# Gated unit of an adaLN block: TensorE and VectorE in source order, the weights' low parts one product behind, the last rows' steps beside the products without down products

## The chip, the cores and the metric

The kernel runs on one core of a Trainium2 chip. The metric is the time of one execution on the device, in microseconds. The engines are TensorE (PE, with its weight loads PEld), VectorE (DVE), ScalarE (ACT), GpSimd (POOL) and SyncE (SP), which here only issues transfers. Each engine works through a queue of its own in order; a semaphore makes an instruction wait for another engine or for a transfer.

## The reference

One block of a transformer with conditioning, on 2048 rows of 576 columns in fp32:

```python
mod = (silu(c) @ w_mod).reshape(c.shape[0], 6, 1, -1)
h = layernorm(x) * (1 + ca) + sa
x = x + ga * attention(h, wqkv, wo)                 # 32 heads of 18, softmax
h = layernorm(x) * (1 + cb) + sb
x = x + gb * ((sigmoid(h @ w_gate) * (h @ w_up)) @ w_down)      # 576 -> 4608 -> 576
```

The last line is the gated unit, the only part that the change touches.

## The kernel before

Attention comes first, up to about 1599 us of the profile. The gated unit fills the rest. It works on two halves of 1024 rows. Each half runs over 18 blocks of 256 of the 4608 inner columns.

**Products.** In a block, gate and up projections together would be eight products of quarter size (two halves of the rows, of the 576 columns and of the block); a scheme of Strassen's kind makes seven of them, in the order `ORDER = (1, 6, 2, 7, 5, 4, 3)` (L43). So the list `seq` (L1074) has 2 x 18 x 7 = 252 products, and `n % 7` is the place in the block, 0 to 6. fp32 values are kept as a high and a low part in fp32r; `product` (L1024) runs 7 matmuls (high by high, high by low, low by high) for the gate and 7 for the up projection, 14 matmuls of 128x512. The activation operands `X[s]` lie in SBUF for the whole half.

**Weights.** `weights_operand` (L991) makes a product's weight tile `w`: GpSimd forms sums and differences of the raw quarters into S1, S2, S3 (L1008), ScalarE casts the high part (L1019), VectorE subtracts for the low part (L1020, L1021), and SP's queue sends the finished tile to the DRAM tensor `ws` (L1022). In the second half the tile is only read back from `ws` (L998). `prepare(n)` (L1094) is called `LOOK = 3` products ahead, and the pool of `w` has four slots. It also loads the raw weights of later blocks.

**What follows a product.** Place 0 (product 1) goes into two banks "x", and ScalarE copies them to p1 (L1206). Place 1 (product 6) goes into "bg" and "bu", and VectorE adds p1 for u2 (L1212). Place 2 (product 2) accumulates on place 0's banks, and `gate` (L1033) follows. Place 3 (product 7) accumulates on bg and bu; L1223 adds for u3. Place 4 (product 5) takes two banks "x", L1228 adds, and a gate follows; place 5 (product 4) accumulates on bg and bu, L1234 and a gate; place 6 (product 3) accumulates on place 4's banks, L1239 and a gate. There are three banks "x", so the next block's place 0 takes a bank that L1239 has to read first. A gate is a chain over two engines: sigmoid on ScalarE (L1037 or L1040), multiply on VectorE (L1038 or L1041), cast of the high part on ScalarE (L1043), subtraction of the low part on VectorE (L1044).

**Down products.** Behind places 1 and 3 stands `down` (L1051) for the block before: eight groups of six matmuls of 288 columns, each into one of three banks "d", each read by one add of VectorE into Oa (L1068).

**Last rows.** Rows 1024 to 2047 still lack the last columns of attention's output product, their layer norm and the activation operands of the second half. The generator `last_rows` (L1108) does this in steps, each up to a `yield`, beside the first half: four transposes and splits of VectorE (L1124 to L1136), products with two adds (L1147, L1150), statistics (L156, L157), scales (L163 to L177, with a square root on ScalarE), normalized rows (L695, with a copy on GpSimd at L698), transposes whose results go to the DRAM tensor `hs` (`ln_spill`, L703), and last the sums and the high and low parts of the operands (`operand_parts`, L717, with the cast L726, the subtractions L728 and L733 and the transfer to `xs`). A step follows every second product (L1241). These steps use the banks "d" as well.

**Who sets the order.** A planner in the framework orders each engine's queue at compile time, by source order as a priority and by its own durations. Inside `tc.manual_schedule(engines=...)` the named engines keep the source order. In the gated unit TensorE alone is named, from product `ORDERED = 56` on, that is from block 8 of the first half (L1197). VectorE, ScalarE, GpSimd and SP are ordered by the planner all the time.

Of the kernel before, what the change touches and what calls it, by code (L numbers as in the profile page):

```python
# [15 lines left out]
F32 = mybir.dt.float32  # L16
# [7 lines left out]
P = 128  # L24
S = 2048
D = 576
# [7 lines left out]
HALF = D // 2  # L34
# [8 lines left out]
ORDER = (1, 6, 2, 7, 5, 4, 3)  # L43
# [5 lines left out]
SINGLE = (0, 1, 16, 17, 18, 19, 20, 27, 28, 29)  # L49
SIDES = ((0, 0), (0, 1), (1, 0), (1, 1))  # L50
TURNED = ((0, 1), (0, 0), (1, 1), (1, 0)), ((0, 1), (1, 1), (0, 0), (1, 0))
ORDERED = 56


@with_exitstack
def tile_block(ctx, tc, x_in, wqkv, wo, w_gate, w_up, w_down, c_in, w_mod, out):
# [102 lines left out]
    def ln_scales(pool, mv, rs):  # L159
        for _ in ln_scales_steps(pool, mv, rs):  # L160
            pass
# [826 lines left out]
    sums = ctx.enter_context(tc.tile_pool(name="sums", bufs=1))  # L988
    wdp = ctx.enter_context(tc.tile_pool(name="wdp", bufs=1))

    def weights_operand(st, k):  # L991

        w = wgp.tile([P, 2, 5, P], F32R, name="w")
        st["w", k] = w
        kept = ws[st["b"], ORDER.index(k)]
        flat = w.rearrange("p v a c -> p (v a c)").bitcast(F32)
        if st["half"] == 1:
            nc.sync.dma_start(flat, kept.bitcast(F32))  # L998
            return
        raw = st["raw"]  # L1000
        A11, A12 = raw[0][:, :, :, 0:P], raw[1][:, :, :, 0:P]
        A21, A22 = raw[0][:, :, :, P:256], raw[1][:, :, :, P:256]

        def put(name, a, b, op):
            if name not in st:
                st[name] = sums.tile([P, 2, 3, P], F32, name=name)
            for v in range(2):
                nc.gpsimd.tensor_tensor(st[name][:, v], a[:, v], b[:, v], op=op)  # L1008

        if k == 6:  # L1010
            put("S1", A21, A22, ALU.add)
            put("S2", st["S1"], A11, ALU.subtract)
            put("S3", A11, A21, ALU.subtract)
        elif k == 3:
            put("S2", A12, st["S2"], ALU.subtract)
        src = {1: A11, 2: A12, 4: A22}.get(k)
        if src is None:
            src = st[{5: "S1", 6: "S2", 7: "S3", 3: "S2"}[k]]
        nc.scalar.copy(w[:, :, 0:3, :], src)  # L1019
        nc.vector.tensor_sub(w[:, :, 3:5, :], src[:, :, 0:2, :], w[:, :, 0:2, :].bitcast(F32))  # L1020
        nc.vector.tensor_sub(w[64:P, :, 2, :], src[64:P, :, 2, :], w[64:P, :, 2, :].bitcast(F32))  # L1021
        nc.sync.dma_start(kept.bitcast(F32), flat)  # L1022

    def product(st, k, acc, first):  # L1024
        s, w = ORDER.index(k), st["w", k]
# [66 lines left out]
        return blocks[half, b]  # L1092

    def prepare(n):  # L1094
        if n < len(seq):
            weights_operand(block(n), seq[n][2])
            at = n % 7
            if at in (1, 3):
                load(n // 7 + 1, at // 2)
# [8 lines left out]
    def last_rows():  # L1108
# [5 lines left out]
        with tc.tile_pool(name="fin", bufs=1, side="right") as pool:  # L1114
            w = pool.tile([P, 2, 2, D], F32R, name="w")
            nc.gpsimd.dma_start(w, wod)
            for t0 in (0, 4):
                od = pool.tile([P, 4, 256], F32, name="od")
                nc.sync.dma_start(od[:, :, 0:192], oend[:, t0 : t0 + 4, :])
                nc.sync.dma_start(od[:, :, 192:256], oend[:, t0 : t0 + 4, 128:192])  # L1120
                yield
                pt = psum()
                for j in range(4):
                    nc.tensor.transpose(pt[:, j * P : (j + 1) * P], od[:, j, 0:P], ident)  # L1124
                oh = pool.tile([P, 512], F32R, name="oh")
                ol = pool.tile([P, 512], F32R, name="ol")
                nc.vector.tensor_copy(oh, pt)
                nc.vector.tensor_sub(ol, pt, oh.bitcast(F32))
                pt = psum()
                for j in range(4):  # L1130
                    nc.tensor.transpose(pt[:, j * P : (j + 1) * P], od[:, j, P:256], ident)
                om = pool.tile([P, 512], F32R, name="om")
                omh = pool.tile([P, 512], F32R, name="omh")
                nc.vector.tensor_copy(om[0:64], pt[0:64])
                nc.vector.tensor_copy(omh[64:P], pt[64:P])
                nc.vector.tensor_sub(om[64:P], pt[64:P], omh[64:P].bitcast(F32))  # L1136
                yield
                for j in range(4):
                    rows = slice(j * P, (j + 1) * P)
                    xt = pool.tile([P, D], F32, name="xt", bufs=2)  # L1140
                    nc.sync.dma_start(xt, x1p[:, t0 + j, :])
                    for h in range(2):
                        cols = slice(h * HALF, (h + 1) * HALF)
                        acc = psum()
                        ts_ = ((oh, 0, 0), (oh, 1, 0), (ol, 0, 0), (om, 0, 1), (om, 1, 1))
                        for n, (a, i, k) in enumerate(ts_):
                            nc.tensor.matmul(  # L1147
                                acc[:, :HALF], a[:, rows], w[:, i, k, cols], start=n == 0, stop=n == 4
                            )
                        nc.vector.tensor_add(xt[:, cols], xt[:, cols], acc[:, :HALF])  # L1150
                    nc.sync.dma_start(x1d[:, t0 + j, :], xt)
                    yield
# [4 lines left out]
        with tc.tile_pool(name="zp2", bufs=1, side="right") as zp:  # L1157
            for ch in (2, 3):
                zs = []
                for t in range(4 * ch, 4 * ch + 4):  # L1160
                    z = zp.tile([P, 2, 384], F32, name="z", bufs=4)
                    x1 = z[:, :, 0:HALF]
                    for g in range(2):
                        nc.sync.dma_start(z[:, g, 0:HALF], x1d[:, t - 8, g * HALF : (g + 1) * HALF])
                    ln_stats(zp, x1, mv2[:, t, :])
                    zs.append(z)
                four = slice(4 * ch, 4 * ch + 4)
                ln_scales(zp, mv2[:, four, :], rs2[:, four])
                for j, z in enumerate(zs):
                    ln_rows(z, 4 * ch + j, z[:, :, 0:HALF], nc.vector)  # L1170
                yield
                yield from ln_spill(zs, ch, psum, zp, modulated)
        with tc.tile_pool(name="xop2", bufs=2) as pool:
# [7 lines left out]
            for i in range(3):  # L1181
                blocks = get()
                for (g, r), t in zip(((0, 0), (0, 1), (1, 0), (1, 1)), blocks):
                    cols = slice(HW + r * 512, HW + (r + 1) * 512)
                    nc.sync.dma_start(t, hs[g, i, :, cols])
                yield from operand_parts(1, i, blocks, parts, nc.scalar.copy, nc.vector, nc.sync)

    def banks(*names):
# [6 lines left out]
    before = None  # L1195
    for n, (hf, b, k) in enumerate(seq):
        if n == ORDERED:  # L1197
            manual.enter_context(tc.manual_schedule(engines={mybir.EngineType.PE}))
        prepare(n + LOOK)
        st = block(n)  # L1200
        if k == 1:
            st["a"] = banks("x", "x")
# [33 lines left out]
        else:  # L1236
# [1 line left out]
            for v in range(2):  # L1238
                nc.vector.tensor_add(half(st["u2"], v), st["c"][v], half(st["u2"], v))  # L1239
            gate(st, st["u2"], 0, 1)  # L1240
        if n >= 5 and n % 2:  # L1241
            next(rows2, None)
        if before is not None and k in (6, 7):
            down(before, k - 6)
        if k == 3:
# [34 lines left out]
```

## Time and profile before

| what | us |
|---|---|
| time, median of 3 runs (2929.81 to 2933.68) | 2929.95 |
| the profiled execution's own time | 2929.86 |
| its span in the profile | 2927.5 |
| start of the gated unit's first product | 1599.17 |
| TensorE busy | 2848.3 |
| VectorE busy | 2218.6 |
| ScalarE busy | 1581.4 |
| GpSimd busy | 649.4 |

A row of a timeline has the start, the duration, the engine, the line, the operation, the output and input tiles (buffer numbers left out), the shapes and the count; a bracket at its end gives the engine's idle time before it and whom it waited for. In the wait list a row names who waited for whom, the total in us, the number of waits and the longest. In a list of groups, the figures behind the bar are busy us, mean ns of one, and the idle time before.

### The profile page before, as it was taken

How to read it: one execution, taken by the hardware profiler on the slowest of the kernel's cores; microseconds unless marked ns; L12 is line 12 of the kernel's file. 1: busy time of each engine (PE TensorE's matmuls, PEld its weight loads, DVE VectorE, ACT ScalarE, POOL GpSimd, SP SyncE). 2: the span in 40 equal slices, each digit the busy share in tenths (PEclk: the TensorE clock that was granted, in tenths of full speed). 3: DMA queues.
4: the chain of work that ended last, by engine and by line, in shares of the span. 5: the costliest groups of instructions: out<-in, count | busy, mean ns of one | idle time of the engine just before them, and what ended most of it. 6: DMA issues, size and time to landing. Idle time of an engine off the chain costs nothing.

```text
span 2927.5 us, 46356 instructions
## 1 busy us (share of the span) xinstructions
PE 2848.3 (97%) x17141; PEld 1879.6 (64%) x17141; DVE 2218.6 (76%) x4023; ACT 1581.4 (54%) x2955; POOL 649.4 (22%) x829
## 2 busy tenths in 40 slices
PE   7999999999999999999999899999999999999998
PEld 6964333333444444444443788877888888888888
DVE  7277888888899988999982878789777555555555
ACT  3216889999987778998788333333332111111111
POOL 3122014544213110761102222233221100000000
PEclk9999999999999999999999999999999999999999
DMA  5344124333212110222125866677556844554443
GB/s 180 120 157 128 52 76 140 133 120 123 84 56 76 35 56 23 101 98 66 52 87 177 284 216 234 231 277 247 207 201 233 301 170 167 167 168 167 159 159 136
DMA packets 136745, 429.25 MB, mean 147 GB/s; under 512 B 18884, under 2 KB 56520, under 8 KB 124232
## 3 DMA queue, kind: packets, MB, share of 16 engines
q1 hardware_dynamic: 120472, 344.99, 35.0%
q0 software_dynamic: 16048, 81.31, 7.9%
q8 instruction: 135, 2.21, 0.3%
q14 instruction: 90, 0.74, 0.1%
HBM read 267.77 MB, written 157.95 MB: 145 GB/s over the span
## 4 chain that ended last, share of the span: by engine, by line
PE 82%; DVE 7%; ACT 4%; DMA 3%; issue 3%; SPq 1%; POOL 0%; POOLq 0%; ACTq 0%; DVEq 0%
PE o L548 16%; PE d L1064 14%; PE x L1028 12%; PE s L446 11%; PE s L927 10%; PE bu L1028 4%; PE bg L1028 4%; PE s L274 4%; ACT p L931 3%; PE s L325 2%; PE s L685 2%; DVE mx L452 1%; DVE w L1020 1%; DMA B<-hs 1%; PE s L572 1%
## 5 line engine op out<-in xcount | busy, mean ns | idle before, releaser
L452 DVE TENSOR_REDUCE mx<-s 128x1 f32<-128x512 f32 x1696 | 1076.6, 684 | 126.3 <-PE s L446 108.3
L931 ACT ACTIVATE p<-s 128x512 f32<-128x512 f32 x2048 | 1068.4, 610 | 146.7 <-PE s L446 75.2
L446 PE MATMUL s<-k,q 54*128 54x512 f32 x1920 | 608.4, 451 | 12.2 <-ACT p L931 6.6
L548 PE MATMUL o<-p,vaug 128*32 128x512 f32 x4096 | 554.8, 607 | 0.5 <-ACT p L931 0.4
L927 PE MATMUL s<-q,k 56*128 56x512 f32 x1920 | 552.6, 425 | 1.3 <-DMA q<-mrows 0.8
L1064 PE MATMUL d<-wd,hh 128*128 128x288 f32 x2304 | 468.3, 297 | 20.8 <-DVE Oa L1068 20.2
L927 PEld LDWEIGHTS s<-q,k 56*128 56x128 f32 x1920 | 260.5, 186 | 295.2 <-DVE mx L452 184.7
L446 PEld LDWEIGHTS s<-k,q 54*128 54x128 f32 x1920 | 273.6, 184 | 250.3 <-ACT p L931 172.3
L1064 PEld LDWEIGHTS d<-wd,hh 128*128 128x128 f32 x2304 | 373.4, 188 | 35.6 <-DVE Oa L1068 26.4
L1068 DVE TENSOR_TENSOR Oa<-Oa,d 128x288 f32<-128x288 f32 x576 | 256.0, 452 | 125.5 <-PE d L1064 120.3
L1064 PE MATMUL d<-wd,hl 128*128 128x288 f32 x1152 | 340.7, 296 | 0.0
L1028 PE MATMUL x<-k,w 128*128 128x512 f32 x1008 | 242.4, 390 | 4.7 <-DVE u L1239 2.4
L1040 ACT ACTIVATE u<-u 128x512 f32<-128x512 f32 x72 | 45.5, 632 | 318.3 <-DVE u L1228 312.1
L1064 PEld LDWEIGHTS d<-wd,hl 128*128 128x128 f32 x1152 | 216.9, 188 | 0.0
L1028 PEld LDWEIGHTS x<-k,w 128*128 128x128 f32 x1008 | 186.7, 188 | 42.5 <-DVE u L1239 3.5
L548 PEld LDWEIGHTS o<-p,vaug 128*32 128x32 f32 x4096 | 83.4, 108 | 163.9 <-issue 151.4
L1037 ACT ACTIVATE sg<-x 128x512 f32<-128x512 f32 x36 | 21.5, 599 | 304.3 <-PE x L1028 304.3
L1070 POOL DMA_DIRECT2D out_dram<-Oa x16 | 8.7, 543 | 606.0 <-DVE Oa L1068 606.0
L455 ACT ACTIVATE over<-s 128x512 f32<-128x512 f32 x176 | 105.1, 597 | 33.5 <-PE s L446 28.4
L1028 PE MATMUL x<-big,w 128*128 128x512 f32 x504 | 120.6, 390 | 1.0 <-issue 1.0
L1028 PE MATMUL x<-w,w 128*128 128x512 f32 x504 | 121.0, 390 | 0.0
L457 DVE CUSTOM_DVE_ANT_0 over<-s,over 128x512 f32<-128x512 f32 x176 | 120.2, 683 | 0.3
(232 smaller groups left out, 3605.1 us busy)
## 6 DMA issues: line engine op xcount, KB each, us to landing
ws<-w SPq DMA_DIRECT2D x126, 640.0 KB
w<-ws SPq DMA_DIRECT2D x126, 640.0 KB
wd<-wds SPq DMA_DIRECT2D x36, 1152.0 KB
k<-kd SPq DMA_DIRECT2D x60, 360.0 KB
wds<-w POOLq DMA_DIRECT2D x18, 1152.0 KB, 4.5
k<-kd SPq DMA_DIRECT2D x60, 180.0 KB
w<-in_B_w_down_dram POOLq DMA_DIRECT2D x18, 576.0 KB, 4.3
q<-qd SPq DMA_DIRECT2D x64, 144.0 KB
```

The source lines that it names most:

```text
L274: nc.tensor.matmul(acc, w, hT[:, t, cols], start=n == 0, stop=n == len(ts_) - 1)
L325: nc.tensor.matmul(acc[:, 0:HALF], hT[:, k, rows], w, start=n == 0, stop=n == len(ts_) - 1,)
L446: nc.tensor.matmul(sp, qs[rows, qt * P : (qt + 1) * P], ks[rows, at * 512 : (at + 1) * 512], start=True, stop=True,)
L452: nc.vector.tensor_reduce(to, sp, axis=AX.X, op=ALU.max)
L455: nc.scalar.activation(over, sp, AF.Relu)
L457: nc.vector.tensor_tensor_reduce(out=over, in0=sp, in1=over, scale=1.0, scalar=LOWEST, op0=ALU.add, op1=ALU.max, accum_out=mx[:, h * n + q ...
L548: nc.tensor.matmul(acc[32 * j : 32 * j + 32, :], vaug[:, kt, (2 * p + h) * VW : (2 * p + h) * VW + 32], probs[2 * c + h], start=kt == 0, s ...
L927: nc.tensor.matmul(sT, ks[rows, kcols], qs[rows, c * 512 : (c + 1) * 512], start=True, stop=True)
L931: state["exp"] = nc.scalar.activation(pr, sT, AF.Exp, scale=SCALE)
L1028: nc.tensor.matmul(acc[v], w[:, v, a, :], X[s][:, b, :], start=first and n == 0, stop=n == 6, skip_group_check=not first,)
L1064: nc.tensor.matmul(acc[:, :HALF], a[:, f, rows], w[:, f, cols], start=n == 0, stop=n == 5)
L1068: nc.vector.tensor_add(Oa[:, t, cols], Oa[:, t, cols], acc[:, :HALF])
```

## The change

Four edits. (1) From product 7 on (block 1 of the first half) TensorE and VectorE both keep the source order; before, TensorE alone did, from product 56. (2) `weights_operand` is split: `weights_high` does the sums and the cast three products ahead, as before, and `weights_low` does VectorE's subtractions and the transfer to `ws` one product later, at the head of the next `prepare`. (3) A step of `last_rows` is taken ahead of the product at places 0, 4, 5 and 6, from product 7 on, and no longer behind every second product; at these places no down products follow. (4) Inside `last_rows` the loads of `x1p` are issued one step ahead, the loads of z and of the blocks from `hs` become steps of their own, and statistics, scales and normalized rows become separate steps, so that there are 56 steps in place of 47.

```diff
--- before.py
+++ after.py
@@ -49,7 +49,8 @@
 SINGLE = (0, 1, 16, 17, 18, 19, 20, 27, 28, 29)
 SIDES = ((0, 0), (0, 1), (1, 0), (1, 1))
 TURNED = ((0, 1), (0, 0), (1, 1), (1, 0)), ((0, 1), (1, 1), (0, 0), (1, 0))
-ORDERED = 56
+ORDERED = 7
+ROWS_FROM = 7
 
 
 @with_exitstack
@@ -988,7 +989,7 @@
     sums = ctx.enter_context(tc.tile_pool(name="sums", bufs=1))
     wdp = ctx.enter_context(tc.tile_pool(name="wdp", bufs=1))
 
-    def weights_operand(st, k):
+    def weights_high(st, k):
 
         w = wgp.tile([P, 2, 5, P], F32R, name="w")
         st["w", k] = w
@@ -1017,9 +1018,18 @@
         if src is None:
             src = st[{5: "S1", 6: "S2", 7: "S3", 3: "S2"}[k]]
         nc.scalar.copy(w[:, :, 0:3, :], src)
+        st["src", k] = src
+
+    def weights_low(st, k):
+
+        if st["half"] == 1:
+            return
+        w, src = st["w", k], st["src", k]
         nc.vector.tensor_sub(w[:, :, 3:5, :], src[:, :, 0:2, :], w[:, :, 0:2, :].bitcast(F32))
         nc.vector.tensor_sub(w[64:P, :, 2, :], src[64:P, :, 2, :], w[64:P, :, 2, :].bitcast(F32))
-        nc.sync.dma_start(kept.bitcast(F32), flat)
+        nc.sync.dma_start(
+            ws[st["b"], ORDER.index(k)].bitcast(F32), w.rearrange("p v a c -> p (v a c)").bitcast(F32)
+        )
 
     def product(st, k, acc, first):
         s, w = ORDER.index(k), st["w", k]
@@ -1092,8 +1102,10 @@
         return blocks[half, b]
 
     def prepare(n):
+        if 0 < n <= len(seq):
+            weights_low(block(n - 1), seq[n - 1][2])
         if n < len(seq):
-            weights_operand(block(n), seq[n][2])
+            weights_high(block(n), seq[n][2])
             at = n % 7
             if at in (1, 3):
                 load(n // 7 + 1, at // 2)
@@ -1135,10 +1147,15 @@
                 nc.vector.tensor_copy(omh[64:P], pt[64:P])
                 nc.vector.tensor_sub(om[64:P], pt[64:P], omh[64:P].bitcast(F32))
                 yield
-                for j in range(4):
+                xts = []
+                for j in range(-1, 4):
+                    if j < 3:
+                        xts.append(pool.tile([P, D], F32, name="xt", bufs=2))
+                        nc.sync.dma_start(xts[-1], x1p[:, t0 + j + 1, :])
+                    if j < 0:
+                        continue
                     rows = slice(j * P, (j + 1) * P)
-                    xt = pool.tile([P, D], F32, name="xt", bufs=2)
-                    nc.sync.dma_start(xt, x1p[:, t0 + j, :])
+                    xt = xts[j]
                     for h in range(2):
                         cols = slice(h * HALF, (h + 1) * HALF)
                         acc = psum()
@@ -1159,13 +1176,15 @@
                 zs = []
                 for t in range(4 * ch, 4 * ch + 4):
                     z = zp.tile([P, 2, 384], F32, name="z", bufs=4)
-                    x1 = z[:, :, 0:HALF]
                     for g in range(2):
                         nc.sync.dma_start(z[:, g, 0:HALF], x1d[:, t - 8, g * HALF : (g + 1) * HALF])
-                    ln_stats(zp, x1, mv2[:, t, :])
                     zs.append(z)
+                yield
+                for j, z in enumerate(zs):
+                    ln_stats(zp, z[:, :, 0:HALF], mv2[:, 4 * ch + j, :])
                 four = slice(4 * ch, 4 * ch + 4)
-                ln_scales(zp, mv2[:, four, :], rs2[:, four])
+                yield from ln_scales_steps(zp, mv2[:, four, :], rs2[:, four])
+                yield
                 for j, z in enumerate(zs):
                     ln_rows(z, 4 * ch + j, z[:, :, 0:HALF], nc.vector)
                 yield
@@ -1183,6 +1202,7 @@
                 for (g, r), t in zip(((0, 0), (0, 1), (1, 0), (1, 1)), blocks):
                     cols = slice(HW + r * 512, HW + (r + 1) * 512)
                     nc.sync.dma_start(t, hs[g, i, :, cols])
+                yield
                 yield from operand_parts(1, i, blocks, parts, nc.scalar.copy, nc.vector, nc.sync)
 
     def banks(*names):
@@ -1195,8 +1215,10 @@
     before = None
     for n, (hf, b, k) in enumerate(seq):
         if n == ORDERED:
-            manual.enter_context(tc.manual_schedule(engines={mybir.EngineType.PE}))
+            manual.enter_context(tc.manual_schedule(engines={mybir.EngineType.PE, mybir.EngineType.DVE}))
         prepare(n + LOOK)
+        if n >= ROWS_FROM and n % 7 in (0, 4, 5, 6):
+            next(rows2, None)
         st = block(n)
         if k == 1:
             st["a"] = banks("x", "x")
@@ -1238,8 +1260,6 @@
             for v in range(2):
                 nc.vector.tensor_add(half(st["u2"], v), st["c"][v], half(st["u2"], v))
             gate(st, st["u2"], 0, 1)
-        if n >= 5 and n % 2:
-            next(rows2, None)
         if before is not None and k in (6, 7):
             down(before, k - 6)
         if k == 3:
```

## The prediction

> **What bounds the kernel now.** I read the page's shares of the engines first, then a table by stage (stretch, length, busy PE, PEld, DVE, ACT, POOL, granted clock, DMA).
>
> ```profile
> span 2927.5 us, 46356 instructions
> PE 2848.3 (97%) x17141; PEld 1879.6 (64%) x17141; DVE 2218.6 (76%) x4023; ACT 1581.4 (54%) x2955; POOL 649.4 (22%) x829
> ...
> 1600.00:1700.00 100.00, 91.68 (x496) 79.00 (x495) 76.80 (x129) 29.87 (x43) 26.84 (x25) 1.00 0.81 274
> 1900.00:2000.00 100.00, 90.99 (x490) 79.52 (x489) 84.81 (x136) 38.06 (x60) 36.06 (x28) 0.98 0.80 279
> 2400.00:2600.00 200.00, 200.00 (x1107) 177.78 (x1106) 113.07 (x196) 35.12 (x58) 0.00 (x0) 1.00 0.51 170
> ```
>
> TensorE is the bound. It has holes in the gated unit's first half and none in the second, so the change, which touches this unit alone, can win only what the first half loses. The timeline says how much that is.
>
> ```profile
> 2500.06 3.35 PE L1028 MATMUL x<-w,w 128*128 128x512 f32 x14
> 2535.02 3.35 PE L1028 MATMUL x<-w,w 128*128 128x512 f32 x14
> ...
> 1631.00 0.59 ACT L1206 COPY p<-x 128x512 f32<-128x512 f32 x1
> 2279.68 0.58 ACT L1206 COPY p<-x 128x512 f32<-128x512 f32 x1
> ...
> 1662.14 0.42 PE L1147 MATMUL d<-w,oh 128*128 128x288 f32 x2
> 1663.46 1.76 PE L1028 MATMUL bg<-big,w 128*128 128x512 f32 x7
> ...
> 1900.63 0.60 PE L710 MATMUL d<-ident,z 128*128 128x128 f32 x4
> 1900.98 3.46 PE L1028 MATMUL x<-k,w 128*128 128x512 f32 x14
> ...
> PE d L1064 <- DVE Oa L1068: 20.2, 22, 2.9
> ```
>
> A block without holes takes 2535.02 - 2500.06 = 34.96 us. Blocks 1 to 17 of the first half run from 1631.00 to 2279.68: 648.7 us, where 17 x 34.96 = 594.3 would do. The last rows' own products are part of the rest: 8 steps of 1.32 us (1662.14 to 1663.46) and 16 groups of four transposes at 0.35 us, 16.2 together. **38.2 us are lost**, the ceiling of any gain. The wait row says to what: TensorE stands in the down products, 22 times, for VectorE's adds into Oa (three banks "d"). Each stall costs more than its idle time:
>
> ```profile
> 2178.81 0.53 PE L1064 MATMUL d<-wd,hh 128*128 128x288 f32 x2 [0.55 <-DVE Oa L1068]
> 2180.15 0.53 PE L1064 MATMUL d<-wd,hh 128*128 128x288 f32 x2 [0.28 <-DVE Oa L1068]
> ...
> 2171.35 0.59 ACT L1206 COPY p<-x 128x512 f32<-128x512 f32 x1
> 2207.81 0.59 ACT L1206 COPY p<-x 128x512 f32<-128x512 f32 x1
> ```
>
> Block 15, without last rows, takes 36.46, that is 1.50 over, with 0.83 idle in two stalls: 0.33 more for each restart.
>
> **The change part by part.** In source order VectorE can no longer fill its own waits. I count a block in places 0 to 6 (products 1, 6, 2, 7, 5, 4, 3; down products behind places 1 and 3). Places 4, 5, 6, 0 have four products and three gates in a row and are VectorE's crowded stretch. Block 15 gives every duration:
>
> ```profile
> 2196.30 3.35 PE L1028 MATMUL x<-k,w 128*128 128x512 f32 x14
> 2205.83 3.33 PE L1028 MATMUL x<-k,w 128*128 128x512 f32 x14
> ...
> 2199.69 0.69 DVE L1228 TENSOR_TENSOR u<-x,u 128x512 f32<-128x512 f32 x1 [0.89 <-PE x L1028]
> 2200.48 0.69 DVE L1041 TENSOR_TENSOR u<-u 128x512 f32<-128x512 f32 x1
> 2201.09 0.69 DVE L1020 TENSOR_TENSOR w<-S,w 128x512 fp32r<-128x512 f32 x1
> 2202.25 0.69 DVE L1044 TENSOR_TENSOR hl<-u,hh 128x512 fp32r<-128x512 f32 x1
> 2202.86 0.68 DVE L1234 TENSOR_TENSOR p<-bg,p 128x512 f32<-128x512 f32 x1
> ...
> 2206.43 0.69 DVE L1239 TENSOR_TENSOR u<-x,u 128x512 f32<-128x512 f32 x1
> ...
> 2201.21 0.62 ACT L1043 CAST hh<-u 128x512 fp32r<-128x512 f32 x1 [0.56 <-DVE u L1041]
> ...
> 1630.37 1.89 PE L1028 MATMUL x<-k,w 128*128 128x512 f32 x7 [2.38 <-DVE u L1239]
> ```
>
> Independent VectorE operations follow each other at 0.60 us, a low part (L1020 and L1021) takes 1.16 (2201.09 to 2202.25), an add and the multiply that needs it 0.79. Between multiply and subtraction of one gate lies ScalarE's cast: 2200.48 to 2201.83, so 1.38 in source order, in which now nothing else may run. Place 4's product starts at 0 and the next block's place 0 at 9.53. The second add of place 4 starts at 3.39 (2199.69), as now. Then in source order: multiply 4.18, subtraction 5.56; place 5: low part 6.16, adds 7.32 and 7.92, multiply 8.72, subtraction 10.10; place 6: low part 10.70, first add 11.86, done 12.55. Now it starts at 10.13 (2206.43), because the low parts lie inside ScalarE's casts. Of three banks "x", the second half of place 0's product takes the one which that add frees. It is due at 9.53 + 1.59 = 11.12, so TensorE waits 1.5 us there: the stall of 1630.37, in every block. With the restart a block without last rows loses 1.85, against 1.50 now. At the down products VectorE is then back in step, and the Oa waits go.
>
> The low part itself, a product later, no longer waits for ScalarE's cast; that wait was VectorE's, with slack, and I count nothing. Its DMA to ws goes down SP's queue one product (3.2 us) later, and four slots "w" turn over behind it:
>
> ```profile
> ACT w L1019 <- DMA ws<-w: 9.0, 3, 4.7
> ...
> L1020 DVE TENSOR_TENSOR w<-S,w 128x512 fp32r<-128x512 f32 x69 | 57.0, 827 | 13.2 <-ACT w L1019 12.7
> ...
> L1150 DVE TENSOR_TENSOR xt<-xt,d 128x288 f32<-128x288 f32 x16 | 7.1, 447 | 0.0
> L1127 DVE CAST oh<-d 128x512 fp32r<-128x512 f32 x2 | 1.4, 685 | 0.0
> L156 DVE BATCH_NORM_STATS2 st<-z 128x6 f32<-128x288 f32 x16 | 6.9, 449 | 2.7 <-DMA z<-x1d 2.6
> L157 DVE BATCH_NORM_AGGREGATE mv<-st 128x2 f32<-128x12 f32 x8 | 1.6, 199 | 0.0
> L695 DVE TENSOR_SCALAR z<-z,mv,rs 128x576 f32<-128x576 f32 x8 | 4.2, 587 | 0.0
> L728 DVE TENSOR_TENSOR ho<-B,ho 128x512 fp32r<-128x512 f32 x14 | 14.5, 1032 | 4.3 <-ACT ho L726 4.3
> ...
> L169 ACT ACT_TABLE_LOAD x2 | 2.6, 1283 | 0.0
> ...
> L698 POOL COPY z<-z 128x192 f32<-128x192 f32 x8 | 4.0, 538 | 18.8 <-DVE z L695 11.1 <-issue 7.7
> ...
> 1966.00:1972.00 6.00, 5.29 (x29) 4.99 (x28) 5.80 (x11) 0.62 (x1) 4.34 (x4) 0.72 0.58 201
> ```
>
> Late slots cost between nothing (a cast is due three products ahead) and 9.0 us more (the present waits again, now on the path); I take nothing and keep 9.0 for the range. The extra loads of x1p and hs are the same DMAs, issued a step earlier in SP's queue: nothing.
>
> The last rows' 56 steps now go into places 0, 4, 5, 6 of blocks 1 to 14, so into the crowded stretch, ahead of each product's own adds. Loss of each block, by the same reckoning:
> - Blocks 1 to 3 (two sets of transposes, eight products with two adds of 0.45): the products give VectorE 1.32 us for 0.9, so 0.7 where they stand alone (block 3) and 2.0 in block 1; in block 2 five splits of 0.69 stand at place 6 and the products of the next step need the last of them: 4.6.
> - Block 4: statistics (8 x 0.43 + 4 x 0.2 = 4.25) at place 4, two table loads of 1.28 ahead of its sigmoid, five short operations (about 1.0 together) at place 5, four L695 (2.1) at place 6; less 1.6 of waiting that they fill, the add at place 6 is 8.6 later, and place 0's transposes wait also for POOL's copy (0.54): 11.8.
> - Block 6: statistics at place 6 make 5.8 at place 0, and loads and short operations 2.1 at the down products: 8.5 with restarts. Block 7: L695 and POOL's copy ahead of place 5's transposes, 2.0. Blocks 5 and 8: transposes give TensorE 0.35 a place, 0.5 each.
> - Blocks 9 to 12: one subtraction L728 (0.60 at least) at places 5 and 6, +1.2: 3.05 each, 12.2. Blocks 13, 14 have two a place: 4.25 each, 8.5.
> - Blocks 15, 16: 3.7. Block 17, low parts ending: 0.4.
>
> Sum: 2.0 + 4.6 + 0.7 + 11.8 + 0.5 + 8.5 + 2.0 + 0.5 + 12.2 + 8.5 + 3.7 + 0.4 = 55.4. The clock adds to it: behind stalls of 1.90 and 0.71 us around 1966 it was 0.72 for 6 us, 1.7 us of work; once each in blocks 4 and 6, 3.4. So 58.8 in place of 38.2: **+20.6**.
>
> [...]
>
> Second half: no low parts, so the add at place 6 starts at 11.86 - 2 x 1.16 = 9.54 and is done at 10.23, 0.9 ahead of its due time: no stall. At the very end, though, the first Oa add stands behind place 6's gate: adds 9.54 and 10.14, multiply 10.94, subtraction 12.32, Oa add 12.92 to 13.37, while the fourth down group could start at 9.53 + 3 x 0.795 = 11.92 (16 groups fill 34.96 - 7 x 3.18): +1.8 with the restart.
>
> Startup (block 0) keeps its free order up to product 7; nothing, with 3 either way. The profiled execution took 2929.86, beside a median of 2929.95. **2929.9 + 20.6 + 1.8 = 2952.3.**
>
> **Rivals.**
> - *The stalls simply go* (faster). VectorE is 85% busy at its fullest and the Oa waits are real. If the add at place 6 ends by 11.12 in most blocks, 1.4 us earlier than I reckon, and the statistics fit in as well, then 20.2 + 22 x 0.33 + 1.7 = 29 are won: 2901. With half of it, 2915. Against it: row 1630.37, the same bank wait even in free order. Chance 0.26.
> - *The order binds little*: VectorE took most operations in source order already, only low parts move. Then within 6 us of 2930. Chance 0.10.
> - *ScalarE, POOL and SP, still ordered by the planner, keep a strict VectorE waiting*: the second half's 0.9 of slack is used up (18 x 0.7 = 13), or L728 at its mean of 1.03 and late ho buffers add 24 x 0.4 = 10, or late slots 9.0. 2962 to 2985, at one or two of them 2970. Chance 0.17.
> [...]
>
> **How the numbers follow.** My forecast, one bank wait in each block and the statistics in the way, covers 2936 to 2962 and has 0.47. Faster by over 0.2% (5.9 us, about what a measurement can tell from no change): 0.26; within: 0.10; slower: 0.64. The range leaves out the lower part of the first rival and the top of the third: 2908 to 2974.
>
> **What would show it.** Right: waits of PE x L1028 for DVE u L1239 in nearly every first-half block, about 1.5 us, and none for Oa; one hole of some 10 us near block 4; blocks of 34.96 in the second half; ScalarE's cast as VectorE's releaser at L1044. Wrong: blocks 15 and 16 below 36.0, no holes at place 0, or holes in the second half.

## The result and the profile after

The change made the kernel slower. Before it takes 2929.88 us (median of 4 runs, 2923.89 to 2933.68), after it **2976.55 us** (median of 4 runs, 2971.55 to 2985.39): a ratio of 1.0164 with a 95% interval of 1.0135 to 1.0194. The forecast was 2952.3 in a range of 2908 to 2974: the direction was right, but 46.7 us were lost where 22.4 were forecast, and the range ends 2.6 us too low.

The profiled execution of after is its slowest run, 2985.39, with a mean granted clock of 0.984. The other three runs of after have 0.987; the profiled run of before has 0.995. So the rows below show some 9 us more loss than the median; 0.003 x 2980 = 9 us is also the estimated worth of the difference in clock.

First the page's shares of the engines, after:

```profile
span 2983.6 us, 46321 instructions
PE 2869.6 (96%) x17141; PEld 1897.4 (64%) x17141; DVE 2195.8 (74%) x4023; ACT 1583.7 (53%) x2955; POOL 638.5 (21%) x829
```

The same 17141 matmuls keep TensorE busy 21.3 us longer (2869.6 against 2848.3), and it idles 34.8 us longer (114.0 against 79.2). The loss has two kinds: holes, and slower work. The stages of after, in the table by stage (stretch, length, busy PE, PEld, DVE, ACT, POOL, granted clock, DMA share, GB/s), are blocks 1 to 17, the first block of the second half, and all the rest:

```profile
1629.17:2327.06 697.89, 642.37 (x3442) 561.22 (x3442) 501.51 (x910) 219.64 (x325) 158.86 (x155) 0.95 0.63 219
2327.06:2368.78 41.72, 36.85 (x196) 32.19 (x195) 19.27 (x35) 6.05 (x10) 8.62 (x16) 0.96 0.89 328
2368.78:2983.60 614.82, 605.64 (x3387) 540.19 (x3385) 335.50 (x596) 103.56 (x171) 4.33 (x8) 1.00 0.48 162
```

The same stages of before:

```profile
1631.00:2279.68 648.68, 626.01 (x3444) 548.22 (x3443) 520.58 (x910) 217.78 (x326) 169.57 (x155) 1.00 0.68 237
2279.68:2314.72 35.04, 35.04 (x195) 31.05 (x194) 19.50 (x34) 6.06 (x11) 7.54 (x14) 1.00 0.93 341
2314.72:2927.50 612.78, 605.04 (x3385) 539.73 (x3383) 338.95 (x595) 103.05 (x171) 5.42 (x10) 1.00 0.48 163
```

Blocks 1 to 17 lose 49.2 us: idle time goes from 22.67 (648.68 - 626.01) to 55.52, which is 32.9 more, and busy time from 626.01 to 642.37, 16.4 more at a granted clock of 0.95. The first block of the second half loses 6.7 and the rest 2.0. Up to block 1, after is 1.8 ahead (1629.17 against 1631.00). Sum: 49.2 + 6.7 + 2.0 - 1.8 = 56.1, the whole difference of the spans.

The wait list of TensorE over the first half and the turn to the second, after:

```profile
PE x L1038 <- DVE u L1261: 41.8, 12, 9.6
...
PE bg L1038 <- DMA w<-ws: 4.9, 1, 4.9
...
PE d L1074 <- DVE Oa L1078: 1.6, 2, 0.9
```

L1038, L1261, L1074 and L1078 are what L1028, L1239, L1064 and L1068 were. The waits for Oa, 20.2 us before, are nearly gone. In their place TensorE waits at place 0 of the next block for the bank "x" that place 6's add has to read.

VectorE's own wait list, from 1597 to 2330 us, shows why the add is late. After, then before (the cast of a gate's high part is `hh`):

```profile
DVE hl L1054 <- ACT hh L1053: 49.5, 69, 1.8
```

```profile
DVE hl L1044 <- ACT hh L1043: 4.4, 13, 0.7
```

VectorE now stands 49.5 us with nothing to do while ScalarE casts, against 4.4, when the planner put other operations there. In block 16, which has no last rows' work, the timeline shows it between two products' adds:

```profile
2283.22 0.69 DVE L1051 TENSOR_TENSOR u<-u 128x512 f32<-128x512 f32 x1
...
2284.60 0.69 DVE L1054 TENSOR_TENSOR hl<-u,hh 128x512 fp32r<-128x512 f32 x1 [0.69 <-ACT hh L1053]
...
2285.21 0.69 DVE L1028 TENSOR_TENSOR w<-raw,w 128x512 fp32r<-128x512 f32 x1
...
2290.91 1.29 DVE L1261 TENSOR_TENSOR u<-x,u 128x512 f32<-128x512 f32 x2
...
2291.66 1.88 PE L1038 MATMUL x<-k,w 128*128 128x512 f32 x7 [1.34 <-DVE u L1261]
```

Multiply to subtraction takes 1.38 with 0.69 of it empty, and the low part, which has lain ready, follows only behind it. The hole of 1.34 stands where 1.5 was forecast.

### The profile page after: what moved, and what is told of

It is laid out like the page before. It is cut to its first block, busy times and chain, and to the rows that moved or that the text cites. A ratio compares the mean times of both kernels' runs of the same rounds, so it can differ in the third digit from the quotient of the medians.

```text
span 2983.6 us, 46321 instructions
## 1 busy us (share of the span) xinstructions
PE 2869.6 (96%) x17141; PEld 1897.4 (64%) x17141; DVE 2195.8 (74%) x4023; ACT 1583.7 (53%) x2955; POOL 638.5 (21%) x829
## 4 chain that ended last, share of the span: by engine, by line
PE 83%; DVE 5%; ACT 4%; DMA 4%; issue 2%; SPq 1%; POOL 0%; POOLq 0%; DVEq 0%; ACTq 0%
PE o L549 16%; PE d L1074 15%; PE x L1038 12%; PE s L447 11%; PE s L928 10%; PE bg L1038 5%; PE bu L1038 5%; PE s L275 4%; ACT p L932 3%; PE s L326 2%; PE s L686 2%; DMA ws<-w 1%; DVE w L1028 1%; DVE mx L453 1%; DVE w L1029 1%
## 5 line engine op out<-in xcount | busy, mean ns | idle before, releaser
L1074 PE MATMUL d<-wd,hh 128*128 128x288 f32 x2304 | 460.8, 295 | 3.0 <-DVE Oa L1078 3.0
L1074 PEld LDWEIGHTS d<-wd,hh 128*128 128x128 f32 x2304 | 373.5, 188 | 9.3 <-DVE Oa L1078 3.7
L1078 DVE TENSOR_TENSOR Oa<-Oa,d 128x288 f32<-128x288 f32 x576 | 258.8, 454 | 163.9 <-PE d L1074 161.3
L1074 PE MATMUL d<-wd,hl 128*128 128x288 f32 x1152 | 340.3, 295 | 0.0
L1038 PE MATMUL x<-k,w 128*128 128x512 f32 x1008 | 261.6, 411 | 44.3 <-DVE u L1261 41.8
L1038 PEld LDWEIGHTS x<-k,w 128*128 128x128 f32 x1008 | 196.5, 199 | 89.6 <-DVE u L1261 47.7
L1074 PEld LDWEIGHTS d<-wd,hl 128*128 128x128 f32 x1152 | 216.2, 188 | 0.0
L1038 PE MATMUL x<-big,w 128*128 128x512 f32 x504 | 121.0, 391 | 0.2 <-DVE u L1250 0.2
L1038 PE MATMUL x<-w,w 128*128 128x512 f32 x504 | 120.5, 390 | 0.0
```

The source lines that it names most:

```text
L1038: nc.tensor.matmul(acc[v], w[:, v, a, :], X[s][:, b, :], start=first and n == 0, stop=n == 6, skip_group_check=not first,)
L1074: nc.tensor.matmul(acc[:, :HALF], a[:, f, rows], w[:, f, cols], start=n == 0, stop=n == 5)
L1078: nc.vector.tensor_add(Oa[:, t, cols], Oa[:, t, cols], acc[:, :HALF])
```

## The experiments

Two theories stood against each other after the result. **Theory A**: VectorE's source order causes the loss: empty cast waits make place 6's add late, and the holes it leaves cost their own length and, behind the longer ones, a slow clock. **The rivals**: the low parts a product later, or the last rows' steps at places 0, 4, 5 and 6, cost the time whatever orders VectorE; or it is the banks. All runs go against before on the same chip, whose median was 2931.24 (first four), 2931.75 (the next three) and 2930.58 (the last three). Idle and busy are TensorE's, from the page of the profiled run.

| kernel | median us | ratio to before (95%) | idle, busy us |
|---|---|---|---|
| VectorE by the planner, rest of the change | 2934.02 | 1.0011 (1.0002 to 1.0020) | 75.6, 2855.9 |
| source order alone, on before | 3004.81 | 1.0249 (1.0234 to 1.0264) | 133.5, 2868.7 |
| four banks "x", two "d" | 3011.07 | 1.0263 (1.0246 to 1.0280) | 134.5, 2877.3 |
| holes fed with matmuls | 2968.83 | 1.0124 (1.0109 to 1.0139) | 85.1, 2878.5 |
| low parts inside four gates | 3016.04 | 1.0284 (1.0267 to 1.0301) | 137.8, 2877.2 |
| the same, steps at places 0 to 3 | 3031.45 | 1.0338 (1.0322 to 1.0353) | 146.3, 2883.1 |
| steps at places 0 to 3 | 2975.49 | 1.0144 (1.0129 to 1.0159) | 113.1, 2855.9 |
| low parts inside the gates of places 5, 6 | 2966.85 | 1.0119 (1.0100 to 1.0139) | 103.9, 2865.7 |
| the same, steps behind the down products | 2969.80 | 1.0133 (1.0118 to 1.0148) | 103.8, 2864.9 |
| planner, steps behind the down products | 2934.88 | 1.0016 (1.0006 to 1.0026) | 77.0, 2853.9 |

**VectorE back to the planner.** After, with TensorE alone in source order:

```diff
-  manual.enter_context(tc.manual_schedule(engines={mybir.EngineType.PE, mybir.EngineType.DVE}))
+  manual.enter_context(tc.manual_schedule(engines={mybir.EngineType.PE}))
```

> The changed kernel with only TensorE in source order from product 7 on; VectorE is left to the planner again. Theory A (VectorE in source order is what costs: its waits inside the gates can't be filled, it reaches place 6's add late, and TensorE waits for bank x): the holes at place 0 go, 2915 to 2940 us, about as before. Rival B (the last rows' steps in the crowded places 4, 5, 6, 0 cost whatever the order is): holes at place 0 stay, 2955 or more. Rival C (the low parts a product later, with their transfers, cost): 2955 or more, with waits for weights.

Measured 2934.02: of the 46.7 us, all but about 3 are gone. Theory A holds, and the rivals that blame the other edits by themselves fall. TensorE keeps its source order from product 7 on in this kernel, so that part of the change is not the cause either. The wait lists of this kernel, TensorE's and VectorE's, are back to those of before:

```profile
PE d L1074 <- DVE Oa L1078: 17.3, 21, 4.2
PE x L1038 <- DVE u L1261: 5.5, 2, 2.9
```

```profile
DVE hl L1054 <- ACT hh L1053: 5.0, 8, 1.7
```

So the 49.5 us of empty cast waits come with the order and go with it.

**Source order alone.** Before, with `ORDERED = 7` and both engines named; low parts and last rows' steps where they were:

```diff
-ORDERED = 56
+ORDERED = 7
-  manual.enter_context(tc.manual_schedule(engines={mybir.EngineType.PE}))
+  manual.enter_context(tc.manual_schedule(engines={mybir.EngineType.PE, mybir.EngineType.DVE}))
```

> The kernel before with only the order changed: TensorE and VectorE in source order from product 7 on; low parts stay with the cast, the last rows' steps stay behind every second product. Theory A: holes at place 0 as in the changed kernel, and VectorE waits besides for ScalarE's cast of the weights at the head of a place: 2960 to 3000 us. Rivals B and C (placing of the steps, later low parts): near before, 2925 to 2940.

Measured 3004.81, 5 above what was expected and 73.6 over before. The order without the other edits is worse than with them: they win back 28 us (3004.81 - 2976.55), and cost about 3 where the planner orders VectorE. Which of them wins it back was not tested apart. The expectation also had VectorE wait for ScalarE's cast of the weights; that came to 6.1 us in four waits. The wait list shows both kinds of lateness in one kernel:

```profile
PE d L1064 <- DVE Oa L1068: 40.1, 12, 11.9
PE x L1028 <- DVE u L1239: 37.0, 15, 4.4
```

**More banks at the place of the wait.** After, with a fourth bank "x" taken from "d":

```diff
-    pd = ctx.enter_context(tc.tile_pool(name="pd", bufs=3, space=PSUM))
+    pd = ctx.enter_context(tc.tile_pool(name="pd", bufs=2, space=PSUM))
-        return [pg.tile([P, 512], F32, name=n, bufs=3 if n == "x" else 1) for n in names]
+        return [pg.tile([P, 512], F32, name=n, bufs=4 if n == "x" else 1) for n in names]
```

> The changed kernel with four banks x and two banks d in place of three and three. If the bank alone is the cause, the 42 us of TensorE's waits for L1261 go and so do the clock's drops behind them: 2925 to 2940 us. Theory A (VectorE is late there by its own chain; the bank only decides where it shows): the waits for L1261 go, but waits for the Oa adds appear at the down products one place later, about 1 to 1.5 us in a block without last rows: 2950 to 2975 us.

Measured 3011.07, above both readings, the theory's 2950 to 2975 too. The wait for the bank is gone from the list, and VectorE's lateness shows at the next place, with 32 waits for Oa; a row from a block without last rows' work stands below the wait:

```profile
PE d L1074 <- DVE Oa L1078: 58.3, 32, 11.5
```

```profile
2283.68 0.53 PE L1074 MATMUL d<-wd,hh 128*128 128x288 f32 x2 [2.25 <-DVE Oa L1078]
```

So a fourth bank "x" does not remove the loss; the lateness shows at another bank. The run is no clean test of the bank alone, because "d" lost one: that the two banks left there let TensorE run less far ahead of VectorE, and so make 2.25 of 1.34, is likely but was not isolated.

**Feeding the holes.** After, with up to 38 extra matmuls of 128x512 into a bank "d" between the two halves of place 0's product, in seven blocks; their results are used by nothing:

```diff
+FEED = {7: 38, 10: 10, 11: 10, 12: 14, 13: 10, 14: 27, 15: 27}
...
+                idle = pd.tile([P, 512], F32, name="d")
+                for j in range(more):
+                    nc.tensor.matmul(idle, w[:, 0, 0, :], X[s][:, 0, :], start=j == 0, stop=j == more - 1)
```

> The changed kernel with extra matmuls of 128x512 into a free bank d between the two halves of place 0's product, where TensorE waits in blocks 7 and 10 to 15: 38, 10, 10, 14, 10, 27, 27 of them at 0.227 us, a little less than the measured waits; their results are not used. If half clock behind those waits is a cost of its own (theory), VectorE's chain and its times stay, the seven matmuls behind take 1.75 us and not 3.2 to 3.4, and the kernel is 8 to 20 us faster than the changed one, 2957 to 2968. If not, it is as the changed kernel, 2972 to 2985.

The feeding does not make the add earlier, so a gain is that of the clock. Measured 2968.83: 7.7 us less than after by the medians, just under what was expected. The profiled run has a clock of 0.994 (after 0.984) and a span 20.0 shorter; the other runs have 0.992 and 0.993 (after 0.987). The product at place 0 of block 13, after and then fed:

```profile
2126.26 3.36 PE L1038 MATMUL x<-k,w 128*128 128x512 f32 x7 [2.67 <-DVE u L1261]
```

```profile
2113.95 2.43 PE L1042 MATMUL d<-k,w 128*128 128x512 f32 x10
2116.78 1.90 PE L1044 MATMUL x<-k,w 128*128 128x512 f32 x7 [0.40 <-DVE u L1267]
```

The hole is filled to 0.40, and the seven matmuls behind it take 1.90 in place of 3.36. The extra matmuls are a group of their own in the list:

```profile
L1042 PE MATMUL d<-k,w 128*128 128x512 f32 x136 | 32.0, 389 | 0.0
```

Without them TensorE is busy 2878.5 - 32.0 = 2846.5, as in before (2848.3): the 21.3 us of slower work have gone with the holes. The profiled run of after is its slowest and that of the fed kernel its fastest, so this pair shows more than the medians do. The medians' 7.7 is also less than an estimate from the clocks (0.0055 x 2976 = 16); where the difference lies was not settled.

**Filling the cast wait by hand.** After, with the low part of places 2, 4, 5 and 6 written inside the gate, between cast and subtraction:

```diff
+    waiting = []
...
+        while waiting:
+            weights_low(*waiting.pop())
...
+            if n - LOOK >= ORDERED and (n - LOOK) % 7 in (2, 4, 5, 6):
+                waiting.append((block(n - 1), seq[n - 1][2]))
+            else:
+                weights_low(block(n - 1), seq[n - 1][2])
```

> The changed kernel, VectorE still in source order, with the low part of places 2, 4, 5, 6 written between a gate's cast on ScalarE and its subtraction, so that it fills the 0.69 us for which VectorE waits there. By the chain of theory A: multiply of place 4 at 4.18, low part 4.78, subtraction 5.94, adds 6.54 and 7.14, multiply 7.94, low part 8.54, subtraction 9.70, add of place 6 10.30 to 10.99, just ahead of the 11.12 at which its bank is due. So no hole at place 0 in blocks 15 and 16 (35.0 to 35.3 us a block in place of 36.64), holes 1.4 us shorter in blocks 9 to 14, 17 x 1.4 = 24 less and some drops of the clock fewer: 2935 to 2955 us. Rival (not the empty waits but VectorE's mere amount of work decides): within 8 us of the changed kernel, 2968 or more.

Measured 3016.04: the expectation failed by over 60 us. The cast wait is filled (1.5 us are left of 49.5), but a chain through two other engines has taken its place: VectorE now waits 27.2 us, in 16 waits, for the sigmoid of place 5. The timeline of block 17:

```profile
2317.84 2.40 POOL L1009 TENSOR_TENSOR S<-S,raw 128x384 f32<-128x384 f32 x2 [12.21 <-DVE w L1029]
2320.28 0.83 ACT L1020 CAST w<-S 128x768 fp32r<-128x768 f32 x1 [2.95 <-POOL S L1009]
...
2321.67 0.69 DVE L1053 TENSOR_TENSOR p<-p 128x512 f32<-128x512 f32 x1 [2.08 <-ACT p L1052]
...
2323.02 1.42 PE L1038 MATMUL x<-k,w 128*128 128x512 f32 x5 [1.14 <-DVE w L1028]
```

GpSimd's next sum waits for the low part, ScalarE's cast waits for that sum at the head of ScalarE's queue, the sigmoid stands behind the cast, and VectorE waits for the sigmoid. Besides, low parts now meet GpSimd's sums:

```profile
2302.76 2.87 POOL L1009 TENSOR_TENSOR S<-raw,raw 128x384 f32<-128x384 f32 x2 [9.05 <-DVE w L1029]
2303.26 1.50 DVE L1028 TENSOR_TENSOR w<-raw,w 128x512 fp32r<-128x512 f32 x1
...
2304.77 1.14 DVE L1029 TENSOR_TENSOR w<-raw,w 64x256 fp32r<-64x256 f32 x1
```

They take 1.50 and 1.14 instead of 0.69 and 0.42 (2285.21 and 2285.93 in after, with no GpSimd operation beside them), and the second ends 0.3 us behind the sum (2305.91 and 2305.63).

**The same, with the steps at places 0 to 3.** The edit above, and:

```diff
-ROWS_FROM = 7
+ROWS_FROM = 10
-        if n >= ROWS_FROM and n % 7 in (0, 4, 5, 6):
+        if n >= ROWS_FROM and n % 7 in (0, 1, 2, 3):
```

> As the kernel with the low parts in the gates, and the last rows' steps at places 0, 1, 2, 3 in place of 0, 4, 5, 6, from product 10 on (so that the loads of z and hs still lie several places ahead). Theory: the crowded stretch has neither empty waits nor the steps' operations, so the waits for L1261 go nearly all (under 8 us in total), what is left are TensorE's waits inside the last rows' own products and transposes: 2905 to 2928 us. Rival (the steps cost as much beside the down products): 2935 or more, with waits for Oa.

Measured 3031.45, the slowest of all and over 100 us above what was expected: the chain above stays (VectorE waits 31.2 us for that sigmoid), and the new places do not help.

**Steps at places 0 to 3, with nothing else.** After, with the two lines of this last diff alone:

> The changed kernel with only the places of the last rows' steps altered, 0, 1, 2, 3 from product 10 on; low parts at the head of each place. Theory: every block keeps the hole of a block without last rows, about 1.34 us idle or 36.6 us a block, the holes of 2.7 to 9.6 us go and with them most drops of the clock: 2930 to 2948 us. Rival (the steps cost the same wherever they stand): 2965 or more.

Measured 2975.49, no different from after (2976.55) and 27 us above the expected range. The wait list says where the expected gain went:

```profile
PE d L1074 <- DVE Oa L1078: 24.6, 14, 6.1
PE x L1038 <- DVE u L1261: 19.4, 15, 2.9
```

The holes at place 0 shrink from 41.8 to 19.4 us, most of them to 1.34, and 24.6 us of waits for Oa come in. The rival of this run was right: with VectorE in source order the steps cost the same at both sets of places.

**Low parts inside the gates of places 5 and 6 only.** The edit of the four gates, with:

```diff
-            if n - LOOK >= ORDERED and (n - LOOK) % 7 in (2, 4, 5, 6):
+            if n - LOOK >= ORDERED and (n - LOOK) % 7 in (5, 6):
```

> The changed kernel with only the low parts of places 5 and 6 written inside the gate; the low part of place 4 is at the head of its place again, so that GpSimd's sum S2, ScalarE's cast of it and the sigmoid of place 5 behind that cast in ScalarE's queue are no longer held back (2.95 and 2.08 us in the kernel with all low parts in the gates). Theory: VectorE then waits for no sigmoid, the add of place 6 ends near 10.6 and the hole at place 0 goes; blocks 15 and 16 take 35.0 to 36.2 us in place of 36.64; 2940 to 2962 us. Rival (any later low part holds up the chain over GpSimd and ScalarE): VectorE still waits about 2 us for ScalarE's sigmoid in every block, 2970 or more.

Measured 2966.85, 5 above the expected range and 10 under after. This is the lowest median of the source-ordered versions, though the runs of the fed kernel and of the next one overlap with it, and still 36 over before. VectorE's empty cast waits fall from 49.5 to 26.1 us, and with the low parts of places 2 and 4 out of the gates the wait for the sigmoid of place 5 falls from 27.2 to 3.5, which bears out the chain above. The hole at place 0 is gone in the blocks without last rows, but waits for Oa are left; whether low parts that meet GpSimd's sums make them was not shown, since in one of these blocks those of places 0 and 1 take 0.69 and 0.42 (from 2276.81 and 2277.96 on):

```profile
PE x L1038 <- DVE u L1268: 17.8, 8, 7.8
PE d L1078 <- DVE Oa L1082: 12.8, 13, 1.8
PE bg L1038 <- DMA w<-ws: 7.7, 1, 7.7
```

**The same, with the last rows' steps behind the down products.** `STEPS` gives how many are taken behind each; the buffers `ho` are three:

```diff
-        if n >= ROWS_FROM and n % 7 in (0, 4, 5, 6):
-            next(rows2, None)
...
+            for _ in range(next(steps, 0)):
+                next(rows2, None)
```

The first of these two runs has VectorE in source order, with the low parts in the gates of places 5 and 6; the second has VectorE by the planner, with the low parts as in after.

> As the kernel before this one, and the last rows' steps taken behind the down products of places 1 and 3, one to three at a time (steps that load stand last in such a group), with three buffers ho. VectorE waits there for the next product anyway. Theory: neither holes at place 0 nor Oa waits in most blocks; TensorE's own waits in the last rows' transposes and products stay: 2912 to 2938 us. If VectorE in source order can't do without the planner's filling, 2945 or more.

> The same places of the last rows' steps with VectorE ordered by the planner, low parts at the head of the places, TensorE in source order from product 7. Theory (the steps in the crowded stretch cost little when the planner may shift them): as the kernel with only TensorE in source order, 2925 to 2940 us; if the Oa waits come from the steps, up to 12 us less, 2918 to 2928.

Measured 2969.80 and 2934.88. The first missed its range by over 30 us, and so fits the run's other reading, that VectorE in source order can't do without the planner's filling; other places were not tried. The second is as expected, and no better than the kernel with the steps at places 0, 4, 5 and 6 (2934.02). No version that was run beats before.

## Why the prediction was right and wrong

**Right: the mechanism.** VectorE's empty cast waits make place 6's add late, TensorE waits for its bank, the waits for Oa go (20.2 to 1.6). The chain came out almost to the digit: L1261 starts 2290.91 - 2279.04 = 11.87 behind place 4's product in block 16, where 11.86 was worked out:

```profile
2253.72 0.59 ACT L1228 COPY p<-x 128x512 f32<-128x512 f32 x1 [0.50 <-PE x L1038]
...
2279.04 3.35 PE L1038 MATMUL x<-k,w 128*128 128x512 f32 x14
...
2290.36 0.59 ACT L1228 COPY p<-x 128x512 f32<-128x512 f32 x1 [0.50 <-PE x L1038]
```

A block without last rows takes 36.64, forecast 34.96 + 1.85 = 36.81. The end of the kernel waits 1.41 in L1074 for Oa, 1.7 with a restart; 1.8 was forecast. Blocks of the second half take 34.96 behind the first one. The wait for L1261 is listed 12 times, at block 1 and at blocks 7 to 17, and not in nearly every block as forecast.

**Wrong: the clock term.** The step that failed is "once each in blocks 4 and 6, 3.4". The forecast had 2.7 to 3.9 us of hole in each of blocks 9 to 14 and charged no clock there; that blocks 4 and 6 alone would pay was the author's estimate, and no run shows it. TensorE's rows behind such holes, after:

```profile
1627.94 3.35 PE L1038 MATMUL x<-k,w 128*128 128x512 f32 x7 [2.92 <-DVE u L1261]
...
1889.43 3.36 PE L1038 MATMUL x<-k,w 128*128 128x512 f32 x7 [9.56 <-DVE u L1261]
...
2006.76 3.17 PE L1038 MATMUL x<-k,w 128*128 128x512 f32 x7 [2.65 <-DVE u L1261]
...
2129.41 3.19 PE L1038 MATMUL bg<-k,w 128*128 128x512 f32 x7
...
2171.26 3.36 PE L1038 MATMUL x<-k,w 128*128 128x512 f32 x7 [6.83 <-DVE u L1261]
```

Seven matmuls take 1.88 behind the hole of 1.34 that block 16 leaves (2291.66 above), and up to 3.36 behind holes of 2.65 or more. Mostly the next seven are slow as well: the row at 2129.41 follows the seven of 2126.26, and takes 3.19 where 1.75 is usual. Behind holes of 2.68 and 3.73 the slow stretch begins late: the first seven take 2.47 and 2.18, the next seven 2.82 and 3.10. There are nine such stretches behind holes of 2.65 to 9.56, from 1627.94 on, of 3.0 to 6.1 us each with a granted clock of 0.50 to 0.66; the holes of blocks 4 and 6 (7.49 and 9.56) make two of them. The missing share of the clock, times their busy time, gives an estimate of some 20 us, 1.4 to 3.1 for each, where 3.4 were put down. A tenth, of 5.12 us at 0.50 from 1714.38 on, follows two holes of 2.01 and 1.63; by the same estimate it is worth 2.6.

The sum of the stage agrees. Blocks 1 to 17 would be busy 17 x 34.96 + 16.2 = 610.5 without any hole; they are busy 642.37, 31.9 more. By these estimates the slow stretches explain some 23 of it, about twenty restarts at 0.33 explain 7, and some 2 stay unexplained. Before has such a remainder too: it is busy 15.5 over 610.5, of which 22 restarts and the drop around 1966 explain 9. The forecast set a sum of single losses, without this remainder, against a measured 38.2 that contains it, and so came out some 6 us low. The median run is 9 us below the profiled one at a clock 0.003 higher, which would leave it an estimated 14 of slow clock; by the medians the fed kernel gave back 7.7. Which holes drop the clock is not given by their length alone. In the fed kernel the first of these places, which is not fed, has a hole of 2.93 and no drop, and a hole of 2.91 in before passes without one too:

```profile
1627.19 1.89 PE L1044 MATMUL x<-k,w 128*128 128x512 f32 x7 [2.93 <-DVE u L1267]
```

```profile
2032.39 0.54 PE L1064 MATMUL d<-wd,hh 128*128 128x288 f32 x2 [2.91 <-DVE Oa L1068]
```

That agrees with runs of one kernel that spread over 14 us at clocks of 0.984 and 0.987. The kernel with the source order alone has both as well: seven matmuls took 3.35 behind a hole of 2.37 (1630.41), and 1.89 behind one of 2.48 (2027.07). What sets a drop was not shown.

**Mis-sized: blocks 6, 13 and 14.** Idle time in blocks 1 to 17 is 55.5. The forecast's 55.4 held some twenty restarts, so about 49 of idle. In blocks 13 and 14 the hole is 6.83, forecast 1.5 + 4 x 0.60 = 3.9, because six subtractions stand at places 4, 5 and 6, not four at two places, and they take more than 0.60. VectorE's timeline of block 13:

```profile
2154.88 2.10 DVE L734 TENSOR_TENSOR ho<-B,ho 32x512 fp32r<-32x512 f32 x2
...
2162.45 1.38 DVE L734 TENSOR_TENSOR ho<-B,ho 32x512 fp32r<-32x512 f32 x2
...
2168.40 2.09 DVE L734 TENSOR_TENSOR ho<-B,ho 32x512 fp32r<-32x512 f32 x2
```

That is 5.6 for 2.4, the 3 us that were missing. In block 6 (9.56, forecast 5.8 behind a clean chain) a transfer is late, and behind a strict VectorE everything waits with it:

```profile
1885.66 0.82 DVE L157 BATCH_NORM_STATS2 st<-z 128x6 f32<-128x288 f32 x2 [4.13 <-DMA z<-x1d]
```

The loads of `z` had become a step of their own. On SP's queue six of these eight transfers are issued only from 1878.95 on:

```profile
1878.95 3.71 SPq L1180 DMA_DIRECT2D z<-x1d  x6
```

One transfer to `ws` and the loads of raw weights stand ahead of them on that queue from 1875.92 on; why they come so late was not isolated. The statistics began at 1880.46. The forecast put nothing for the loads of `x1p` and `hs`, and had no term for late loads of `z`, which cost these 4.13. Block 4, on the other side, came out at 8.9 of idle where 11.8 with a restart, so 11.5, was forecast.

**Not forecast: the turn of the halves.** The forecast's "no stall" for the second half missed 6.7 us in its first block: TensorE waits 4.87 for a weight tile read back from `ws`, and then runs slowly.

```profile
2333.43 2.95 PE L1038 MATMUL bg<-k,w 128*128 128x512 f32 x7 [4.87 <-DMA w<-ws]
```

On SP's queue of after the last tile goes out to `ws` between the first reads:

```profile
2310.09 0.32 SPq L999 DMA_DIRECT2D w<-ws  x1
...
2317.45 0.32 SPq L1030 DMA_DIRECT2D ws<-w  x1
2319.07 19.75 SPq L999 DMA_DIRECT2D w<-ws  x5
```

In before the writes end at 2261.6 and the first read follows at 2261.73. That late low parts push these transfers into each other is likely, but was only read from the traces. The wait is 7.7 in one of the experiments, and absent in the two with VectorE by the planner and in the one without late low parts.

**What stays open**: how the loss of the median run divides between clock and restarts, which only profiled runs show, the remainder of busy time that both kernels have, which of the other edits wins back 28 us under the source order, and the cause of the wait for `ws`. The rivals of the prediction: "the stalls simply go" was half right, since the Oa waits did go, but were paid back at place 0; "keep a strict VectorE waiting" named the size (2962 to 2985) by the wrong terms, except that a late transfer and stretched subtractions, which it allowed for, took part.

## What to carry to other kernels

Before an in-order engine is tied to the source order, count the waits inside its own chains (here 0.69 us for every cast of a gate) and see what fills them now. Here these waits came to 49.5 us of VectorE, and leaving VectorE to the planner again won 42 us of time (2976.55 - 2934.02), because place 6's add is a deadline for TensorE; the two numbers need not agree elsewhere, since a part of the time is slow clock. Moving the work by hand moved the lateness to the next deadline here, or through a third engine's queue; look for who waits for the moved operation, and behind whom that one stands. And price a hole of TensorE with its clock: in after nine holes of 2.65 to 9.56 us cost an estimated 1.4 to 3.1 us each beyond their length, because the clock fell; behind a hole of 2.93 in the fed kernel it did not fall, and seven matmuls took 1.89 against 1.75.

## What the runs showed of the hardware

- Behind holes of TensorE of 2.65 to 9.56 us in after, nine stretches of 3.0 to 6.1 us had a granted clock of 0.50 to 0.66. Seven matmuls of 128x512 took 3.17 us behind the hole of 2.65 and up to 3.36 behind others, against 1.88 behind a hole of 1.34. With the source order alone they took 3.35 behind a hole of 2.37; holes of 2.91 in before and 2.93 in the fed kernel passed without a drop. With holes filled by matmuls whose results nobody uses, the mean clock was 0.992 to 0.994, against 0.984 to 0.987, and the median 7.7 us lower.
- VectorE's subtraction for a low part, from two SBUF tiles, took 1.50 us beside a GpSimd sum (2303.26, low parts inside four gates), and 0.69 with none beside it (2285.21, after); the smaller one 1.14 and 0.42. The pair (2303.26 to 2305.91) ends about as the sum's two operations do (2302.76 to 2305.63). What holds it up was not shown.
